# Polynomial-sketch attention and a rational-activation layer: 28 accumulating transfers, coefficients loaded by GpSimd, and a new order of all steps

## The chip, the cores and the metric

One core of a Trainium2 chip runs the whole program. The metric is the device time of one execution in microseconds, the median of several runs. Five engines work from queues of their own, each strictly in order: TensorE (PE, with its weight loads PEld), VectorE (DVE), ScalarE (ACT), GpSimd (POOL) and SyncE (SP). SP and POOL issue most of the DMAs.

## What is computed

Two stages in a row. The first is linear attention with a polynomial sketch, for 4 batches of 4 heads, 1088 positions and 32 channels. The second is a two-matrix layer (128 to 2048 to 128) whose activation is a cubic over a quadratic.

```python
def phi(x):
    a = np.einsum('rd,bhsd->bhsr', S1, x)          # r = 8
    b = np.einsum('rd,bhsd->bhsr', S2, x)
    return np.einsum('bhsi,bhsj->bhsij', a, b).reshape(*x.shape[:-1], r * r)
q_p, k_p = phi(q), phi(k)
kv = np.einsum('bhsf,bhsd->bhfd', k_p, v)
z = np.sum(k_p, axis=2)
num = np.einsum('bhsf,bhfd->bhsd', q_p, kv)
den = np.einsum('bhsf,bhf->bhs', q_p, z)[..., None] + 1e-06
x = (num / den)                                    # then (4352 tokens, 128)

h = x @ w_in                                       # 128 -> 2048
P = a[0] + a[1] * h + a[2] * h**2 + a[3] * h**3
Q = 1.0 + np.abs(b[0]) * np.abs(h) + np.abs(b[1]) * h**2
out = (P / (Q + 1e-06)) @ w_out                    # 2048 -> 128
```

## The kernel before

**An order written out by hand.** The string `ORDER` lists every step of the kernel, some 650 of them, by short names. The kernel walks through it once and emits each step's instructions. So each engine's queue is the list of its own steps in that order, and only waits between engines shape the time. A step's name gives its kind, its number, sometimes a part, and sometimes the engine (`a` for ScalarE, `d` for VectorE).

**Attention.** `Kb.…` are the steps of the keys of batch b: `T` turns them (VectorE), `s` forms the sketches (TensorE), `c` copies one factor out of PSUM, `f` multiplies the factors (VectorE), `p` multiplies with the values (TensorE), `k` keeps the result. `Qb.y.…` are those of the queries of one slice of a batch: `T`, `sk`, `c`, then `dw` and `dr` (written to DRAM and read back repeated, by SP's DMAs), `f` (VectorE), `p` (TensorE), `pl` (adds 1e-6 to the denominator), `r` (reciprocal, VectorE), `x` (quotient, VectorE), `b` (turned back by TensorE), `kk` (into the ring `xT`).

**The layer.** It is cut into 21 units (`UNITS`): a range of tokens and a range of the sixteen 128-wide slices of the hidden layer. Units 3 to 16 are 512 tokens by 8 slices, which is 4096 columns per partition; the first and the last ones are smaller. The steps of unit i, in the order of the data:

| step | engine | what it does |
|---|---|---|
| H | TensorE | h = w_in x, 1024 columns of PSUM at a time (two buffers `h_ps`) |
| E | ScalarE | evacuates them to `hh` in bf16 (three buffers) |
| U, W, Y | VectorE | u = abs(h) by a bit mask; w = b1 u + b0; w = w u, so that Q = 1 + w |
| L, X | ScalarE | ln of (w + 1 + 1e-6), then exp of its negative: r = 1/Q |
| S | VectorE | s = h r |
| P, V | VectorE | g = a3 h + a2; g = g h |
| G | VectorE | g = g s |
| Or, Os, Og | TensorE | gather: w_out times a0 with r, w_out times a1 with s, w_out with g |
| ST, OUT | ScalarE or VectorE, SP | out of PSUM, and to DRAM |

Three variants save work on one engine at another's cost:

- Units of `TWO` (6, 7, 8, 10, 12, 14, 15): behind V, step `A` adds a1 to g by an accumulating DMA that GpSimd issues, out of a DRAM tensor `ones` that holds a1 everywhere (fp32). Then the matmuls of Os aren't needed. There are two transfers of 512 KB per unit.
- Units of `SQ` and `ABS` (5, 9, 13): ScalarE squares h (`D`, with the root of b1 as scale) and forms b0 abs(h) (L530); `M` adds the two by an accumulating DMA. This takes the place of U, W and Y. `u` has one buffer, so the next unit's u waits until the transfer has read it.
- Units of `FOUR` (11, 13, 16, 17): VectorE forms s h and s h h (`B`, `C`) in place of P, V and G, and TensorE gathers four times (Or, Os, Om, On), the last two with weights scaled by a2 and a3 (steps w6 and w7).

So before there are 20 accumulating transfers, 14 for A and 6 for M. `w` and `r` and `s` have two buffers each, `g` four, the output tile two. P is done in halves of 2048 columns, as is D.

**The start.** SP issues the first loads (`I…`), among them the coefficients a and b (`I8`, L180 and L182). `AB0` takes the absolute of b and the root of b1 on ScalarE. `Z` steps are idle turns of TensorE on zeros.

Of the kernel before, what the change touches and what calls it, by code (L numbers as in the profile page):

```python
# [22 lines left out]
TWO = (6, 7, 8, 10, 12, 14, 15)  # L23
SQ = (5, 9, 13)
ABS = (5, 9, 13)
FOUR = (11, 13, 16, 17)
# [3 lines left out]
WIDE = {'U': 4096, 'W': 4096, 'Y': 4096, 'V': 4096, 'S': 4096, 'G': 4096, 'L': 4096}  # L30
# [8 lines left out]
I0 I11 I1 I2 K0.T0 SS0 Z10 K0.s0 K0.T1 K0.T2 K0.c0.a K0.f0 Q0.0.T Z3 K0.s1 Z3 Q0.0.sk I3 K0.p0 I8 F1.k I7 I9 I4 I5  # L39
K0.c1.a K0.f1 Q0.0.c.a Q0.0.f Q0.1.T K0.p1 K0.k0.d Q0.2.T K1.T0 Q0.1.sk Q0.0.p Q0.2.sk K1.s0 K1.T1 Q0.1.c.a  # L40
Q0.0.pl.a Q0.0.r Q0.0.x K1.T2 Q0.2.c.a Z2 Q0.0.b K1.s1 I6 I10 Q0.2.dw Q0.1.f K1.c0.a Q0.3.T Q0.0.kk.a H0.0 w2.d
K1.f0 AB0 w0.a w4.a K1.c1.d F1.q K1.f1 E0.0 U0.0 H1.0 Q0.3.sk E1.0 F1.v Q0.2.dr Q0.1.p H2.0 P0.0.d Q0.3.c.d W0.0
Q0.1.pl.d Y0.0 Q0.1.r U1.0 Q1.0.T V0.0 Q0.1.x W1.0 Q1.1.T w3.a P1.0.a E2.0 w1.a Y1.0 V1.0 H2.1 Q1.0.sk Q0.1.b
K1.p0 K1.p1 E2.1 Q1.0.c.a w5.a Q0.1.kk.a L0.0 P2.0.d Q0.2.f Q0.2.p Q0.2.pl.a K1.k0.a X0.0 Q1.2.T U2.0 Q0.2.r
Q1.1.sk Q1.2.sk Q0.3.dw F2.k Q1.0.dw Q0.2.x Q0.2.b Or0.0 W2.0 S0.0 V2.0 K2.T0 G0.0 Y2.0 Q0.2.kk.a L1.0 Q1.1.c.a
X1.0 H3.0 E3.0 H3.1 E3.1 K2.s0 K2.c0.a H3.2 L2.0 Q1.2.c.a E3.2 F2.q Q0.3.dr Q1.1.dw S1.0 K2.T1 P3.0.d G1.0 Q2.0.T
K2.f0 Q2.1.T H3.3 E3.3 Q0.3.f U3.0 K2.T2 W3.0 Q2.2.T Y3.0 Os0.0 H4.0 H4.1 Og0.0 Q2.0.sk Q1.0.dr Q1.2.dw Q1.1.dr
K2.s1 Q0.3.p X2.0 E4.0 P3.1.a H4.2 Q0.3.pl.d K2.c1.d Q1.0.f K2.f1 Q2.0.c.a E4.1 Q1.0.p H4.3 Q1.0.pl.d Q0.3.r
Q1.0.r Q0.3.x Q0.3.b L3.0 Q1.0.x S2.0 E4.2 Q0.3.kk.a Or1.0 Q1.0.b Os1.0 Os2.0 E4.3 Q1.2.dr F2.v Q2.0.dw Q1.0.kk.a
H5.0 H5.1 X3.0 E5.0 Q2.1.sk E5.1 Q2.1.c.a D5.0 Q2.2.sk H5.2 H5.3 E5.2 Q2.2.c.a E5.3 P4.0.d Q1.1.f U4.0 P4.1.d V3.0  # L50
W4.0 G2.0 Y4.0 S3.0 V4.0 Q1.2.f Og1.0 H6.0 Or2.0 F3.q F3.k Q2.1.dw Q2.0.dr Q2.2.dw Q1.1.p K2.p0 K2.p1 Q1.2.p Og2.0
H6.1 Q1.1.pl.d P5.0.d K2.k0.d Q1.1.r Q1.2.pl.d P5.1.d Q1.2.r Q3.0.T ST2.d Q1.2.x Q1.1.x D5.1 W5.0 E6.0 L4.0 Or3.0
H6.2 Q1.1.b Q1.2.b E6.1 X4.0 Q1.1.kk.a E6.2 H6.3 Os3.0 Q1.2.kk.a E6.3 Q3.0.sk G3.0 K3.T0 Q3.1.T P6.0.d Q2.0.f V5.0
S4.0 Q2.0.p Q3.1.sk Q3.0.c.a M5.0 L5.0 H7.0 E7.0 Og3.0 H7.1 H7.2 Q2.1.dr F3.v Q3.0.dw AW0 OUT2 Q2.2.dr X5.0 E7.1
K3.T1 Q2.0.pl.d G4.0 U6.0 P6.1.d W6.0 Q2.0.r Q3.2.T Y6.0 Q2.0.x S5.0 Q2.1.f V6.0 Q3.1.c.a E7.2 L6.0 Or4.0 H7.3
H8.0 E7.3 E8.0 Os4.0 Og4.0 H8.1 X6.0 E8.1 ST4.a Q3.1.dw Q3.0.dr OUT4 H8.2 H8.3 Or5.0 Q2.0.b K3.s0 Q2.1.p U7.0
P7.0.d W7.0 K3.T2 Y7.0 G5.0 P7.1.d S6.0 Q2.2.f E8.2 L7.0 Q2.0.kk.a E8.3 X7.0 H9.0 E9.0 H9.1 Q2.1.pl.a V7.0 U8.0
P8.0.d Q2.1.r Q3.0.f E9.1 K3.c0.a A6.0 D9.0 Os5.0 H9.2 H9.3 E9.2 E9.3 A7.0 Q2.1.x W8.0 K3.f0 Y8.0 K3.s1 K3.c1.a
S7.0 P8.1.d K3.f1 G6.0 Or6.0 Q2.1.b H10.0 Og5.0 H10.1 K3.p0 K3.p1 Q2.2.p D9.1 W9.0 E10.0 L8.0 E10.1 K3.k0.a X8.0
P9.0.d V8.0 P9.1.d Og6.0 H10.2 H10.3 E10.2 ST6.a E10.3 M9.0 Q2.1.kk.d V9.0 Q2.2.pl.d G7.0 P10.0.d S8.0 Q2.2.r  # L60
Q3.2.sk Q3.0.p U10.0 Q2.2.x H11.0 H11.1 L9.0 E11.0 Or7.0 Q2.2.b H11.2 Q3.0.pl.a Q3.2.c.d W10.0 Q3.0.r P10.1.d
Y10.0 E11.1 X9.0 A8.0 E11.2 H11.3 E11.3 Og7.0 Q3.0.x S9.0 U11.0 Q2.2.kk.d V10.0 Q3.0.b H12.0 H12.1 W11.0 G8.0
# [12 lines left out]
L20.0 Z4 Or18.0 OUT17 X20.0 Or19.0 Os18.0 Os19.0 Og18.0 Or20.0 S20.0 Os20.0 G19.0 Og19.0 G20.0 Og20.0 ST20 OUT20
# [4 lines left out]
def kernel(  # L80
# [81 lines left out]
    def early(n):  # L162
# [7 lines left out]
        elif n == 2:  # L170
            nc.sync.dma_start(out=q0[:, 0:QA], in_=q0_src[:, 0:QA])
        elif n == 3:
            load_v(0)
        elif n < 7:
            c, e = ((0, 512), (512, 1024), (1024, d_ff))[n - 4]
            nc.sync.dma_start(out=w_in_sb[:, c:e], in_=moe_w_in[:, c:e])
        elif n == 7:
            nc.sync.dma_start(out=q0[:, QA:S], in_=q0_src[:, QA:S])
        elif n == 8:
            nc.sync.dma_start(out=a_sb, in_=bass.AP(tensor=moe_a.tensor, offset=moe_a.offset,  # L180
                                                    ap=[[0, 128]] + list(moe_a.ap)))
# [63 lines left out]
    root1 = consts.tile([128, 1], FP, name="root1")  # L245
# [3 lines left out]
    a1, a2, a3 = a_sb[:, 1:2], a_sb[:, 2:3], a_sb[:, 3:4]  # L249
    w_sb = [big.tile([128, nf, d_model], BF, name=f"w_out_{i}") for i in range(3)] + [None, None]  # L250
    xT = big.tile([d_model, RING], FP, name="xT")
    if TWO:
        a1_sb = consts.tile([128, 128], FP, name="a1_sb")
        ones = dram.tile([128, 2048], FP, name="ones", bufs=1)
# [260 lines left out]
    def evac(i, part):  # L515
        c, ce = part * HW, min((part + 1) * HW, width(i))
        nc.scalar.copy(out=at(i, "hh", c, ce), in_=live[i]["h", part][:, :ce - c])  # L517
# [9 lines left out]
    def d_w(i, k, eng="d"):  # L527
        c = span(i, "W", k)
        if i in ABS:
            nc.scalar.activation(out=at(i, "u", *c), in_=at(i, "hh", *c), func=ACT.Abs, scale=ab0)  # L530
# [10 lines left out]
    def square(i, k):  # L541
        c = span(i, "D", k)
        nc.scalar.activation(out=at(i, "w", *c), in_=at(i, "hh", *c), func=ACT.Square, scale=root1)  # L543
# [127 lines left out]
    def w_part(x, eng):  # L671
        if x >= 6:
            t = feature_tile(x - 6)[:, 0:4].rearrange("p t h i j -> p (t h i j)").bitcast(BF)
            t = w_sb[x - 3] = t.rearrange("p (f d) -> p f d", f=nf)
            if eng == "d":
                nc.vector.tensor_scalar(out=t, in0=w_sb[2], scalar1=a_sb[:, x - 4:x - 3], scalar2=None, op0=AX.mult)
            else:
                nc.scalar.activation(out=t, in_=w_sb[2], func=ACT.Copy, scale=a_sb[:, x - 4:x - 3])
# [7 lines left out]
        if y == 2:  # L686
            copy(eng, o, t)
        elif eng == "d":
            nc.vector.tensor_scalar(out=o, in0=t, scalar1=a_sb[:, y:y + 1], scalar2=None, op0=AX.mult)
        else:  # L690
            nc.scalar.activation(out=o, in_=t, func=ACT.Copy, scale=a_sb[:, y:y + 1])

    def written(_):
        nc.sync.dma_start(out=ones.rearrange("p (a c) -> p a c", c=128),
                          in_=a1_sb[:, None, :].broadcast_to([128, 16, 128]))

    def absolute(_):
        if TWO:
# [56 lines left out]
```

## Time and profile before

| | us |
|---|---|
| median of 3 runs | 257.76 (257.49 to 258.58) |
| span of the profiled execution | 255.8 |
| TensorE busy in it | 249.8 |
| VectorE busy in it | 243.3 |
| ScalarE busy in it | 232.2 |
| accumulating transfers of ones, issue to landing, least / median / most | 6.9 / 9.7 / 12.4 |
| accumulating transfers of u, issue to landing, least / median / most | 4.6 / 6.9 / 9.1 |

The profile is of one execution. Its page gives each engine's busy time and share, the chain of work that ended last, and groups of instructions by line and form, as count, busy time in us, mean of one in ns, and idle time of the engine before them. A view by stretches gives busy time and count for each engine in each, then the granted TensorE clock (1.00 throughout), the share of the DMA engines and GB/s. A view in order of time gives start, duration, engine, line and tiles. TensorE's ends are modelled, so that a busy TensorE is not one at its peak. The span leaves out what lies around the program; the median of the runs is 1.96 us above it.

### The profile page before, as it was taken

How to read it: one execution, taken by the hardware profiler on the slowest of the kernel's cores; microseconds unless marked ns; L12 is line 12 of the kernel's file. 1: busy time of each engine (PE TensorE's matmuls, PEld its weight loads, DVE VectorE, ACT ScalarE, POOL GpSimd, SP SyncE). 2: the span in 40 equal slices, each digit the busy share in tenths (PEclk: the TensorE clock that was granted, in tenths of full speed). 3: DMA queues.
4: the chain of work that ended last, by engine and by line, in shares of the span. 5: the costliest groups of instructions: out<-in, count | busy, mean ns of one | idle time of the engine just before them, and what ended most of it. 6: DMA issues, size and time to landing. Idle time of an engine off the chain costs nothing.

```text
span 255.8 us, 6273 instructions
## 1 busy us (share of the span) xinstructions
PE 249.8 (98%) x2699; PEld 178.0 (70%) x2702; DVE 243.3 (95%) x242; ACT 232.2 (91%) x176; POOL 22.5 (9%) x46
## 2 busy tenths in 40 slices
PE   8999999999999999999999999999999999999993
PEld 3677746646866575666756656689566599999982
DVE  3699999999999999999999999999999999999992
ACT  2179989999999999999999999999899899999980
POOL 4000000000300040202200100220002020000000
PEclk9999999999999999999999999999999999999999
DMA  6999375649884669395995695399008575120100
GB/s 189 278 324 259 108 219 158 149 86 292 192 193 133 196 135 124 74 112 85 152 140 146 140 117 97 35 143 190 6 0 93 75 86 81 31 54 3 44 23 21
DMA packets 22618, 31.85 MB, mean 125 GB/s; under 512 B 2880, under 2 KB 15808, under 8 KB 22592
## 3 DMA queue, kind: packets, MB, share of 16 engines
q0 software_dynamic: 2880, 10.49, 30.1%
q1 hardware_dynamic: 19424, 20.90, 29.5%
q8 instruction: 21, 0.34, 0.5%
q10 hardware_dynamic: 288, 0.08, 0.1%
q14 instruction: 5, 0.04, 0.0%
HBM read 31.39 MB, written 4.26 MB: 139 GB/s over the span
## 4 chain that ended last, share of the span: by engine, by line
PE 96%; ACT 1%; DVE 0%; issue 0%; DVEq 0%
PE h_ps L511 47%; PE out_ps L616 34%; PE att_ps L426 3%; PE out_ps L197 3%; PE att_ps L330 2%; PE att_ps L454 2%; PE att_ps L299 1%; PE att_ps L366 1%; PE h_ps L376 1%; PE h_ps L299 1%; ACT hh L517 0%; ACT ln L575 0%; ACT w_out L265 0%; PE att_ps L197 0%; PE att_ps L322 0%
## 5 line engine op out<-in xcount | busy, mean ns | idle before, releaser
L511 PE MATMUL h_ps<-xT,w_in_sb 128*128 128x512 f32 (+1 forms) x320 | 126.2, 537 | 0.0
L511 PEld LDWEIGHTS h_ps<-xT,w_in_sb 128*128 128x128 f32 x320 | 57.5, 190 | 41.7 <-issue 36.6
L517 ACT CAST hh<-h_ps 128x1024 bf16<-128x1024 f32 x68 | 69.3, 1045 | 3.7 <-PE h_ps L511 2.2
L575 ACT ACTIVATE ln<-w 128x4096 f32<-128x4096 bf16 (+2 forms) x21 | 63.1, 3006 | 0.2 <-DVE w L553 0.2
L579 ACT ACTIVATE r<-ln 128x4096 bf16<-128x4096 f32 (+2 forms) x21 | 63.0, 2999 | 0.1
L583 DVE TENSOR_TENSOR s<-hh,r 128x4096 bf16<-128x4096 bf16 (+2 forms) x21 | 39.5, 1883 | 0.3 <-ACT r L579 0.2
L616 PEld LDWEIGHTS <-r 128*128 128x128 bf16 x544 | 31.7, 98 | 6.0 <-issue 5.1
L616 PEld LDWEIGHTS <-g 128*128 128x128 bf16 x544 | 31.4, 98 | 5.8 <-issue 5.1
L616 PE MATMUL out_ps<-w_out,r 128*128 128x128 bf16 x544 | 33.7, 219 | 0.0
L553 DVE TENSOR_TENSOR w<-w,u 128x4096 bf16<-128x4096 bf16 (+2 forms) x18 | 32.5, 1806 | 0.1
L571 DVE TENSOR_TENSOR g<-g,hh 128x4096 bf16<-128x4096 bf16 (+2 forms) x17 | 30.3, 1783 | 0.0
L587 DVE TENSOR_TENSOR g<-g,s 128x4096 bf16<-128x4096 bf16 (+2 forms) x17 | 30.2, 1781 | 0.0
L616 PEld LDWEIGHTS <-s 128*128 128x128 bf16 x448 | 25.9, 98 | 3.6 <-issue 3.4
L616 PE MATMUL out_ps<-w_out,g 128*128 128x128 bf16 x416 | 26.0, 219 | 0.0
L567 POOL DMA_DIRECT2D g<-ones x14 | 13.8, 1157 | 103.7 <-PE out_ps L616 39.1
L616 PE MATMUL out_ps<-w_out,s 128*128 128x128 bf16 x320 | 19.8, 219 | 0.0
L538 DVE TENSOR_SCALAR w<-u,b_abs 128x4096 bf16<-128x4096 bf16 (+2 forms) x17 | 19.3, 1136 | 0.0
L558 DVE TENSOR_SCALAR g<-hh,a_sb 128x2048 bf16<-128x2048 bf16 (+1 forms) x24 | 19.0, 793 | 0.0
L524 DVE TENSOR_SCALAR u<-hh 128x4096 uint16<-128x4096 uint16 (+2 forms) x17 | 17.3, 1015 | 0.1
L543 ACT ACTIVATE w<-hh,root 128x2048 bf16<-128x2048 bf16 x6 | 12.2, 2031 | 0.0
L549 POOL DMA_DIRECT2D w<-u x6 | 5.4, 1058 | 74.4 <-ACT u L530 74.4
L530 ACT ACTIVATE u<-hh,b_abs 128x4096 bf16<-128x4096 bf16 x3 | 11.1, 3713 | 0.0
(81 smaller groups left out, 207.1 us busy)
## 6 DMA issues: line engine op xcount, KB each, us to landing
g<-ones POOLq DMA_DIRECT2D x14, 512.0 KB, 9.7
w<-u POOLq DMA_DIRECT2D x6, 512.0 KB, 6.9
a_all<-sk_d SPq DMA_DIRECT2D x6, 352.0 KB
b_all<-sk_d SPq DMA_DIRECT2D x12, 176.0 KB
v_sb<-in_v_dram SPq DMA_DIRECT2D x12, 144.0 KB
k_sb<-in_k_dram SPq DMA_DIRECT2D x3, 544.0 KB
q_sb<-in_q_dram SPq DMA_DIRECT2D x3, 544.0 KB
out_dram<-out_sb SPq DMA_DIRECT2D x19, 64.0 KB
```

What stands on the lines that cost most here:

```text
L511: nc.tensor.matmul(t[:, (x - part * m) * tl:(x - part * m + 1) * tl], lhsT=w_in_sb[:, (f0 + x) * 128:(f0 + x + 1) * 128], rhs=xT[:, p:p + ...
L517: nc.scalar.copy(out=at(i, "hh", c, ce), in_=live[i]["h", part][:, :ce - c])
L524: nc.vector.tensor_scalar(out=at(i, "u", *c).bitcast(U16), in0=at(i, "hh", *c).bitcast(U16), scalar1=0x7FFF, scalar2=None, op0=AX.bitwise_and)
L538: nc.vector.tensor_scalar(out=at(i, "w", *c), in0=at(i, "u", *c), scalar1=ab1, scalar2=ab0, op0=AX.mult, op1=AX.add)
L553: nc.vector.tensor_mul(out=at(i, "w", *c), in0=at(i, "w", *c), in1=at(i, "u", *c))
L558: nc.vector.tensor_scalar(out=at(i, "g", *c), in0=at(i, "hh", *c), scalar1=a3, scalar2=a2, op0=AX.mult, op1=AX.add)
L571: nc.vector.tensor_mul(out=at(i, "g", *c), in0=at(i, "g", *c), in1=at(i, "hh", *c))
L575: nc.scalar.activation(out=ln_sb[:, :ce - c], in_=at(i, "w", c, ce), func=ACT.Ln, bias=1.0 + 1e-6)
L579: nc.scalar.activation(out=at(i, "r", c, ce), in_=ln_sb[:, :ce - c], func=ACT.Exp, scale=-1.0)
L583: nc.vector.tensor_mul(out=at(i, "s", *c), in0=at(i, "hh", *c), in1=at(i, "r", *c))
L587: nc.vector.tensor_mul(out=at(i, "g", *c), in0=at(i, "g", *c), in1=at(i, "s", *c))
L616: nc.tensor.matmul(outs[t0][:, m * 128:(m + 1) * 128], lhsT=z[:, m * 128:(m + 1) * 128], rhs=w, start=first and j == 0 and m == 0, stop=le ...
```

## The change

- `TWO` becomes (6, 8, 10, 11, 12, 13, 14, 15), `SQ` (5, 7, 9, 11, 13, 15), `FOUR` (16, 17); `ABS` goes. That makes 28 accumulating transfers: 16 of A and 12 of M.
- In units of SQ, u is now the plain abs(h) by VectorE's bit mask, the square's scale is the root of b1/b0, and the factor b0 enters in Ln as its scale (`scale0`).
- `ones` is bf16 instead of fp32. So that a1 may be rounded, `nearest` (steps KA0 to KA2) forms the ratio k of the rounded a1 to a1; a2 and a3 are multiplied by it, and the weights of g by its inverse.
- The coefficients are loaded by GpSimd's queue instead of SP's.
- P and D are done in one step of 4096 columns (except P of unit 3). E may be done by VectorE; seven of 68 are.
- `ORDER` is another one, throughout.

```diff
-TWO = (6, 7, 8, 10, 12, 14, 15)
-SQ = (5, 9, 13)
-ABS = (5, 9, 13)
-FOUR = (11, 13, 16, 17)
+TWO = (6, 8, 10, 11, 12, 13, 14, 15)
+SQ = (5, 7, 9, 11, 13, 15)
+FOUR = (16, 17)
+HALF = (3,)
...
-WIDE = {'U': 4096, 'W': 4096, 'Y': 4096, 'V': 4096, 'S': 4096, 'G': 4096, 'L': 4096}
+WIDE = {'U': 4096, 'W': 4096, 'Y': 4096, 'V': 4096, 'S': 4096, 'G': 4096, 'L': 4096, 'P': 4096, 'D': 4096}
...
-I0 I11 I1 I2 K0.T0 SS0 Z10 K0.s0 K0.T1 K0.T2 K0.c0.a K0.f0 Q0.0.T Z3 K0.s1 Z3 Q0.0.sk I3 K0.p0 I8 F1.k I7 I9 I4 I5
...
-S7.0 P8.1.d K3.f1 G6.0 Or6.0 Q2.1.b H10.0 Og5.0 H10.1 K3.p0 K3.p1 Q2.2.p D9.1 W9.0 E10.0 L8.0 E10.1 K3.k0.a X8.0
-P9.0.d V8.0 P9.1.d Og6.0 H10.2 H10.3 E10.2 ST6.a E10.3 M9.0 Q2.1.kk.d V9.0 Q2.2.pl.d G7.0 P10.0.d S8.0 Q2.2.r
...
+I0 K0.T0 I11 Z10 SS0 I1 K0.s0 Z1 K0.T1 K0.c0.d I8 AB0 RT0 K0.T2 K0.s1 Z3 K0.f0 I2 I3 Q0.0.T Q0.0.sk Q0.0.c.a K0.c1.d
...
+ST4.a V6.0 V7.0 E8.0.a Q2.2.dw H8.2 E8.2.a Q2.0.kk.a S6.0 Q2.1.p Or5.0 L7.0 H9.1 E9.1.a P8.0.d V8.0 H9.0 E9.0.a U8.0.d
+W8.0.d Q3.0.sk A6.0 Y8.0 K3.T0 G6.0 Q2.2.dr Q2.1.pl.a Q2.1.r Q2.1.x Og5.0 X7.0 A8.0 H9.3 H9.2 E9.3.a E9.2.a U9.0.d
+Q3.0.c.a P9.0.d K3.s0 H10.2 S7.0 D9.0 Q2.2.f F3.v M9.0 K3.s1 K3.c1.a L8.0 H10.3 E10.3.a Q3.1.sk Q3.2.T K3.c0.a Or6.0
+Os5.0 E10.2.d Og6.0 K3.f1 OUT2 Q3.1.c.a X8.0 H10.0 E10.0.a V9.0 ST6.a Q2.1.b Q2.1.kk.a K3.f0 H10.1 S8.0 G8.0 E10.1.a
...
-            nc.sync.dma_start(out=a_sb, in_=bass.AP(tensor=moe_a.tensor, offset=moe_a.offset,
+            nc.gpsimd.dma_start(out=a_sb, in_=bass.AP(tensor=moe_a.tensor, offset=moe_a.offset,
...
-        a1_sb = consts.tile([128, 128], FP, name="a1_sb")
-        ones = dram.tile([128, 2048], FP, name="ones", bufs=1)
+        a1_sb = consts.tile([128, 256], BF, name="a1_sb")
+        ones = dram.tile([128, 2048], BF, name="ones", bufs=1)
...
-    def evac(i, part):
+    def evac(i, part, eng="a"):
...
-        nc.scalar.copy(out=at(i, "hh", c, ce), in_=live[i]["h", part][:, :ce - c])
+        copy(eng, at(i, "hh", c, ce), live[i]["h", part][:, :ce - c])
...
-        if i in ABS:
-            nc.scalar.activation(out=at(i, "u", *c), in_=at(i, "hh", *c), func=ACT.Abs, scale=ab0)
-            return
...
-        nc.scalar.activation(out=at(i, "w", *c), in_=at(i, "hh", *c), func=ACT.Square, scale=root1)
+        nc.scalar.activation(out=at(i, "w", *c), in_=at(i, "hh", *c), func=ACT.Square, scale=root)
...
-        nc.scalar.activation(out=ln_sb[:, :ce - c], in_=at(i, "w", c, ce), func=ACT.Ln, bias=1.0 + 1e-6)
+        nc.scalar.activation(out=ln_sb[:, :ce - c], in_=at(i, "w", c, ce), func=ACT.Ln, bias=1.0 + 1e-6,
+                             scale=scale0 if i in SQ else 1.0)
...
+        by = k_inv if y == 2 else a_sb[:, y:y + 1]
...
     def absolute(_):
-        if TWO:
-            nc.gpsimd.tensor_copy(out=a1_sb, in_=a1.broadcast_to([128, 128]))
         nc.scalar.activation(out=b_abs, in_=b_sb, func=ACT.Abs)
-        if SQ:
-            nc.scalar.activation(out=root1, in_=ab1, func=ACT.Ln, bias=tiny)
-            nc.scalar.activation(out=root1, in_=root1, func=ACT.Exp, scale=0.5)
+        nc.gpsimd.tensor_scalar(out=scale0, in0=ab0, scalar1=1e-12, scalar2=None, op0=AX.max)
+
+    def nearest(n):
+        if n == 0:
+            nc.gpsimd.tensor_copy(out=a1_sb, in_=a1.broadcast_to([128, 256]))
+            nc.gpsimd.tensor_scalar(out=zero, in0=a1_sb[:, 0:1], scalar1=0.0, scalar2=None, op0=AX.is_equal)
+            nc.gpsimd.tensor_add(out=near[:, 0:1], in0=a1, in1=zero)
+            nc.gpsimd.tensor_add(out=near[:, 1:2], in0=a1_sb[:, 0:1], in1=zero)
+        elif n == 1:
+            nc.vector.reciprocal(out=near_inv, in_=near)
+        else:
+            nc.gpsimd.tensor_mul(out=a_k[:, 0:1], in0=near[:, 1:2], in1=near_inv[:, 0:1])
+            nc.gpsimd.tensor_mul(out=a_k[:, 1:2], in0=near[:, 0:1], in1=near_inv[:, 1:2])
+            nc.gpsimd.tensor_mul(out=a_k[:, 2:4], in0=a_sb[:, 2:4], in1=a_k[:, 0:1].broadcast_to([128, 2]))
+
+    def square_root(_):
+        nc.scalar.activation(out=ln_b[:, 0:1], in_=scale0, func=ACT.Ln)
+        nc.scalar.activation(out=ln_b[:, 1:2], in_=ab1, func=ACT.Ln, bias=tiny)
+        nc.scalar.mul(ln_b[:, 0:1], ln_b[:, 0:1], -0.5)
+        nc.scalar.activation(out=root, in_=ln_b[:, 1:2], func=ACT.Exp, scale=0.5, bias=ln_b[:, 0:1])
```

## The prediction

> **What bounds the kernel now.** I read the page first (busy shares and the chain that ended last), then the busy time by stretches of 30 us, then VectorE's instructions in order of time, then the groups by form for prices. The page:
>
> ```profile
> span 255.8 us, 6273 instructions
> ...
> PE 249.8 (98%) x2699; PEld 178.0 (70%) x2702; DVE 243.3 (95%) x242; ACT 232.2 (91%) x176; POOL 22.5 (9%) x46
> ...
> PE 96%; ACT 1%; DVE 0%; issue 0%; DVEq 0%
> ```
>
> By this page TensorE is the bound: 98% busy, and 96% of the chain. The stretches (columns PE, PEld, DVE, ACT, POOL) say more:
>
> ```profile
> 30.00:60.00 30.00, 30.00 (x216) 16.61 (x216) 29.94 (x38) 29.07 (x30) 0.00 (x0) 1.00 0.64 177
> ...
> 90.00:120.00 30.00, 30.00 (x297) 19.80 (x295) 29.68 (x24) 30.00 (x23) 5.73 (x6) 1.00 0.71 106
> ...
> 150.00:180.00 30.00, 30.00 (x367) 22.90 (x365) 29.78 (x24) 29.44 (x18) 3.52 (x4) 1.00 0.75 116
> ...
> 210.00:240.00 30.00, 30.00 (x384) 28.17 (x383) 29.89 (x19) 29.85 (x19) 0.00 (x0) 1.00 0.27 50
> ```
>
> From 30 to 240 us all three engines are full. VectorE lies idle 1.1 us in these 210. Of its 12.5 us outside busy time some 6.6 lie in the first 20 us and 4.6 behind its last work. So work taken from TensorE alone buys nothing: the end moves with VectorE's queue, and ScalarE's stands close behind it.
>
> **How VectorE's queue is priced.** Its instructions in order of time (start, duration):
>
> ```profile
> 171.03 0.69 DVE L267 COPY out_sb<-out_ps 128x512 f32<-128x512 f32 x1
> 171.63 2.29 DVE L592 TENSOR_TENSOR g<-s,hh 128x4096 bf16<-128x4096 bf16 x1
> 173.95 2.29 DVE L599 TENSOR_TENSOR s<-g,hh 128x4096 bf16<-128x4096 bf16 x1
> 176.16 0.17 DVE L435 TENSOR_SCALAR den<-att_ps 128x12 f32<-128x12 f32 x1
> ...
> 209.21 1.24 DVE L524 TENSOR_SCALAR u<-hh 128x4096 uint16<-128x4096 uint16 x1
> 210.49 1.34 DVE L538 TENSOR_SCALAR w<-u,b_abs 128x4096 bf16<-128x4096 bf16 x1
> 211.75 2.28 DVE L587 TENSOR_TENSOR g<-g,s 128x4096 bf16<-128x4096 bf16 x1
> ```
>
> An instruction that doesn't read what the one ahead of it wrote starts 0.08 to 0.09 us before that one's end: 173.95 + 2.29 - 176.16 = 0.08; 210.49 + 1.34 - 211.75 = 0.08. One that does starts 0.03 us after it: B11 at 171.63 + 2.29 = 173.92, C11 at 173.95; U16 at 209.21 + 1.24 = 210.45, W16 at 210.49. This holds all along VectorE's trace, wherever no other engine is waited for. So a step costs its duration less 0.085, and 0.12 more if it stands right behind the step that it reads. I call that a **pair**. Prices:
>
> ```profile
> L553 DVE TENSOR_TENSOR w<-w,u 128x4096 bf16<-128x4096 bf16 x12 | 27.4, 2280 | 0.1
> L538 DVE TENSOR_SCALAR w<-u,b_abs 128x4096 bf16<-128x4096 bf16 x12 | 16.1, 1341 | 0.0
> L524 DVE TENSOR_SCALAR u<-hh 128x4096 uint16<-128x4096 uint16 x12 | 14.7, 1221 | 0.1
> L558 DVE TENSOR_SCALAR g<-hh,a_sb 128x2048 bf16<-128x2048 bf16 x23 | 18.5, 804 | 0.0
> L311 DVE TENSOR_TENSOR k_p<-att_ps,b_sk 128x1024 f32<-128x1024 f32 x3 | 3.6, 1209 | 0.0
> L530 ACT ACTIVATE u<-hh,b_abs 128x4096 bf16<-128x4096 bf16 x3 | 11.1, 3713 | 0.0
> ...
> L543 ACT ACTIVATE w<-hh,root 128x2048 bf16<-128x2048 bf16 x6 | 12.2, 2031 | 0.0
> ```
>
> **The change on VectorE, step by step.**
> - Units 7, 11, 15 get the squared denominator and lose W and Y: 3 x (1.26 + 2.20) = -10.4.
> - Units 5, 9, 13 get U back from ScalarE: 3 x 1.14 = +3.4.
> - Units 11, 13 exchange B and C for V and G, four steps of 2.29 either way: 0.
> - P: before 23 halves at 0.72 and one quarter at 0.455, 17.0; after 12 whole steps (W's row stands for them, 1.255), two halves, three quarters, 17.9: +0.9.
> - Seven evacuations of 1024 columns from PSUM (E10.2, E12.1, E13.0, E14.1, E15.2, E16.0, E17.2) come from ScalarE. No row has this copy; the nearest, a product of the same width out of PSUM, is 1.21, and L689's cast of that width out of SBUF is 0.71: 7 x 0.63 to 1.13 = 4.4 to 7.9. I take 7.9, the row that reads PSUM too.
> - Small steps, by their rows less 0.085: U1, U20 (0.42 each), W1 (0.54), two kvz copies (0.29), two sketch copies (0.34, 0.32), five pieces of xT (2.1 together), four den (0.16), ST2 (0.39) and one more turn-out (0.69) leave, -4.9; the weight scalings w6, w7 (0.72) leave, -1.3; w1, w4, w5 (0.71) and a reciprocal (0.2) come, +2.0. Together -4.2.
>
> Sum without pairs: -2.4.
> - Pairs. Taking VectorE's steps alone out of each order, 10 of before stand right behind what they read. After has 54: P>V 12, S>G 9, U>W 9, r>x 8, W>Y 7, pl>r 4, others 5. 44 more at 0.12 is 5.3; some six lie in the first 20 us or the last 10, where VectorE waits anyhow, so 4.6 at least. I take +4.9.
>
> VectorE: **+2.5 us** (bounds -3.2, with the cheap evacuation and only half the pairs showing, and +2.9, with all 44).
>
> **ScalarE**, whose queue covers about 4 us of mid-kernel waits: three Abs of 3.71 leave, -11.1; squares go from six halves of 2.03 to six whole ones (the Abs row, 3.71), +10.1; seven evacuations leave, -7.3; weights, copies, den, U and W come, +8.6; the start's small ones +0.5. Ln of six units takes a per-partition scale: Ln with such a bias took 0.295 where Exp without took 0.203, so +0.5. Six more pairs at 0.13, +0.8. Sum some +1.6 with the overlap of more instructions: hidden, since VectorE's end moves further. If VectorE weren't later, up to 1.6 of it would show.
>
> **TensorE**: three groups of 32 gather matmuls fewer (two each in units 11 and 13, one more in unit 7), 96 x 0.056 = -5.4 (32 take 1.79 in the chain); eight idle turns fewer, -3.0. Worth nothing where VectorE is full.
>
> **Transfers.** 28 accumulating transfers instead of 20, issued two by two in 1.8 us on POOL, which is free. ScalarE's own work between the square and the logarithm that waits for the join was 14.8 to 15.4 us; it's now 10.8 to 13.4. Joins landed 4.6 to 9.1 us after issue, the second half issued 0.9 later, so 10.0 at worst: 0 for L, with 0.8 to spare. Behind a late join stand all evacuations in ScalarE's queue, then TensorE's two h_ps buffers. Of ones, V to G has 12.5 us of VectorE's work or more against 12.4 + 0.9 at worst, and the source is halved: 0 (0.8 once if not). U behind a join waits for it as well (one u buffer): 9.4 us or more of VectorE's work and the join's own issue; 0 to 0.6.
>
> The Trainium skill's "SBUF — State Buffer" (section "SBUF: two separate sides") says that descriptors of GpSimd's DMAs can't be written while VectorE runs in a two-port mode. The trace has issues of 0.86 to 1.99 us, so something holds them at times; by the rule joins would land later, which is the third rival below.
>
> **The start.** The coefficients' two DMAs go from SP (issued at 5.03 and 5.51) behind POOL's sketch weights, which end at 5.88; at 0.86 to 1.99 each they are issued by 7.6 to 9.9. On SP a_sb landed 3.4 us after its issue. Abs of b now stands ahead of Q0.0.c in ScalarE's queue, with four small ones (0.2 to 0.3) behind it: Q0.0.c starts at about 11.3 to 13, where it was 10.32. VectorE has Q0.1.T, Q0.2.T and two K0 copies to do meanwhile. So 0 to 1.5; I take +0.3. SP's later loads go 0.9 earlier. OUT8 goes to the end of SP's queue and keeps one of two out_sb buffers; ST10 to ST16 then wait for the store before them, which has some 15 us: 0.
>
> **Sum**: 255.8 + 2.5 + 0.3 = 258.6 for the profiled execution. The median of the runs, 257.76, is 1.96 above its span, so 257.76 + 2.8 = **260.6 us**.
>
> **Rivals.**
> 1. *Pairs cost nothing* in that queue (0.12): then -2.4 + 0.3, so 255.7, or up to 257.3 where ScalarE's +1.6 shows. For: the page's rows know no such price, and each is small. Against: ten of ten pairs before show it.
>    The Trainium skill, "VectorE: DVE Perf Modes" (The DRAIN you can't avoid), says that a semaphore after each of eight copies cost nothing extra. The trace disagrees by 0.12 us a pair.
> 2. *TensorE is the bound after all* (0.05): the chain says so. Then -5.4 alone: 252.4. Against it: VectorE idle 1 us in 210.
> 3. *A join lands late* (0.10): with more pairs, all six land like the worst of ones, 12.4 + 0.9 = 13.3. The gaps to L are 12.2, 12.4, 11.6, 13.4, 10.8, 10.8: 8.7 us of waits in ScalarE's queue, of which 4.9 are covered (4.0 that it waits now, 2.5 more behind VectorE, less 1.6). It decides from 10.8 us on: 260.6 + 3.8 = 264.4. For: the worst landing seen; against: joins landed sooner than ones each time.
> 4. *One cost is smaller* (0.11): evacuations at 0.63 give -0.7 in all, 257.1; half the pairs covered by waits give +0.5, 258.3. For: neither was seen in this place; against: the nearest rows.
>
> The forecast has 0.62, spread over 259.1 to 262.5. A measurement of this kernel tells 0.5% from no change, 1.3 us: slower is above 259.05, the forecast and rival 3, 0.72; faster is rival 2 and seven twelfths of rival 1, 0.12; the rest, 0.16, is the same. The range 256.4 to 263.5 leaves out rival 2, half of 1 and half of 3.
>
> **What would show it.** In VectorE's order of time: P8 then V8, S8 then G8 and U8, W8, Y8 with +0.03 us between, others -0.08; its busy time near 245 and its idle time in mid-kernel still about 1 us; E10.2 at 1.2 us; TensorE with some 8 us more idle time; Ln behind a join not waiting for a DMA. Wrong if VectorE shows idle time of several us in mid-kernel released by ScalarE or a DMA, or if pairs start like others.

## The result, and the profile after

The changed kernel takes **266.18 us** (median of 4 runs, 264.69 to 266.86), beside 257.62 (257.26 to 258.58) for the kernel before on the same chip: 1.0317 times as long, interval 1.0275 to 1.0358. That is 8.6 us slower. The profiled execution is the shortest of the four (264.69), with a span of 262.9 against 255.8: 7.1 of the 8.6 us can be looked at in it.

The page of the changed kernel, the lines that answer to those shown of before:

```profile
span 262.9 us, 6073 instructions
...
PE 249.0 (95%) x2597; PEld 172.0 (65%) x2598; DVE 244.7 (93%) x223; ACT 234.0 (89%) x184; POOL 32.9 (13%) x63
...
PEclk9999999999999799999999999999999999999999
...
DVE 44%; PE 16%; issue 15%; DMA 14%; ACT 8%; POOL 1%; SPq 1%; DVEq 0%; ACTq 0%
```

The chain, 96% TensorE before, now runs through VectorE and through DMAs (14%). One slice of 40 has a granted TensorE clock under 0.9. By stretches of 30 us (columns PE, PEld, DVE, ACT, POOL, clock, DMA share, GB/s):

```profile
30.00:60.00 30.00, 28.76 (x267) 16.63 (x266) 29.62 (x35) 27.24 (x30) 0.00 (x0) 1.00 0.57 164
60.00:90.00 30.00, 27.67 (x265) 16.71 (x264) 26.81 (x22) 27.15 (x21) 1.88 (x2) 0.94 0.62 149
90.00:120.00 30.00, 30.00 (x303) 19.82 (x302) 29.69 (x25) 28.89 (x22) 5.69 (x6) 1.00 0.78 153
...
150.00:180.00 30.00, 29.28 (x302) 20.36 (x300) 28.63 (x21) 29.97 (x19) 6.94 (x8) 1.00 0.70 142
...
210.00:240.00 30.00, 29.86 (x346) 26.70 (x345) 29.75 (x18) 29.89 (x15) 1.79 (x2) 1.00 0.30 61
```

VectorE is nearly full but for two stretches: 3.2 us are missing from 60 to 90, 1.4 from 150 to 180. Its list of waits (what it waited for: us in all, times, longest) names them:

```profile
DVE k_p L299 <- DMA k_sb<-in_k_dram: 4.2, 2, 2.7
DVE u L531 <- DMA w<-u: 3.0, 1, 3.0
DVE s L585 <- ACT r L581: 1.7, 2, 1.3
DVE a_all L419 <- ACT a_all L272: 1.4, 1, 1.4
```

The first and the last lie in the first 13 us, and VectorE waited about as long at the start before (5.6 us in all in the first 25 us, 5.9 now). The two in the middle are new, but for 0.2 us at an S step. This is the first of them in order of time, with only the rows that bear on it (start, duration, engine, line, and in brackets what ended the wait):

```profile
66.68 1.88 POOL L550 DMA_DIRECT2D w<-u  x2 [52.44 <-DVE g L559]
67.66 0.35 SPq L132 DMA_DIRECT2D q_sb<-in_q_dram  x1
68.05 0.46 SPq L128 DMA_DIRECT2D k_sb<-in_k_dram  x1
...
79.14 1.23 DVE L531 TENSOR_SCALAR u<-hh 128x4096 uint16<-128x4096 uint16 x1 [3.00 <-DMA w<-u]
80.41 1.35 DVE L539 TENSOR_SCALAR w<-u,b_abs 128x4096 bf16<-128x4096 bf16 x1
81.67 2.29 DVE L585 TENSOR_TENSOR s<-hh,r 128x4096 bf16<-128x4096 bf16 x1
...
84.05 1.93 ACT L272 CAST hh<-h_ps 128x1024 bf16<-128x1024 f32 x2 [1.20 <-DVE s L585]
85.11 5.40 PE L518 MATMUL h_ps<-xT,w_in_sb 128*128 128x512 f32 x8 [2.33 <-ACT hh L272]
```

It reads as a chain of five. POOL issues the two joining transfers of unit 5. One us later SP issues the queries and keys of the last batch, 544 KB each. The second join lands 11.7 us after its issue (the first took 5.7), and U6, which writes the one `u` buffer that the join reads, waits 3.0 us for it. Behind U6 in VectorE's queue stand W6 and then S4, the last reader of an `hh` buffer, so ScalarE's copies out of PSUM wait 1.2 and TensorE 2.3. Then eight matmuls of H take 5.40 us; without that wait eight take 3.49 (at 109.05 in the same trace's chain). The finer stretches (same columns) show why:

```profile
82.00:84.00 2.00, 0.78 (x28) 0.64 (x22) 2.00 (x2) 0.84 (x1) 0.00 (x0) 1.00 1.03 181
84.00:86.00 2.00, 0.89 (x2) 0.38 (x3) 2.00 (x1) 1.96 (x3) 0.00 (x0) 0.84 0.83 282
86.00:88.00 2.00, 2.00 (x4) 0.94 (x3) 2.00 (x3) 2.00 (x2) 0.00 (x0) 0.50 0.50 152
88.00:90.00 2.00, 2.00 (x5) 0.80 (x4) 2.00 (x4) 2.00 (x2) 0.00 (x0) 0.81 0.00 1
```

TensorE stands idle for 2.33 us, from 82.78 to 85.11. By the clock records of the trace the granted clock is then 0.50 from 85.34 to 88.76, which these stretches show as 0.84, 0.50 and 0.81.

The groups that stand for the prediction's prices (busy us, mean ns):

```profile
L274 DVE CAST hh<-h_ps 128x1024 bf16<-128x1024 f32 x7 | 8.4, 1204 | 0.0
L559 DVE TENSOR_SCALAR g<-hh,a_k 128x4096 bf16<-128x4096 bf16 x12 | 16.0, 1335 | 0.0
L576 ACT ACTIVATE ln<-w,scale 128x4096 f32<-128x4096 bf16 x6 | 22.4, 3738 | 1.1 <-DMA w<-u 1.1
```

**VectorE's account.** All rows of VectorE's timeline, added up: the end of the last one is its first start (0.85 us), the durations, the overlaps of neighbours (rows that start over 0.03 us before the end of the one ahead), the small gaps up to 0.12 us (pairs), and the longer waits. The three lower rows are experiments told below.

```
kernel                 end     durations  overlaps (rows)  small gaps (rows)  waits
before                 251.9   260.7      -17.4 (203)      +0.8 (17)           6.9
after                  259.2   256.5      -11.9 (145)      +2.4 (59)          11.3
e6 before, 17 pairs    254.1   260.0      -15.4 (190)      +1.2 (33)           7.5
e11 after, S4 first    257.5   256.5      -11.7 (144)      +2.6 (61)           9.3
e7 loads, start        255.6   256.4      -11.5 (142)      +2.4 (61)           7.5
```

From before to after: durations -4.2, overlaps and gaps +7.1, waits +4.4, together +7.3, which is the span's +7.1 within 0.2.

### The profile page after: what moved, and what is told of

It reads as the page before. It is cut to its first block, busy times and chain, and to the rows that moved or that the text cites. A ratio compares the mean times of both kernels' runs of the same rounds, so it can differ in the third digit from the quotient of the medians.

```text
span 262.9 us, 6073 instructions
## 1 busy us (share of the span) xinstructions
PE 249.0 (95%) x2597; PEld 172.0 (65%) x2598; DVE 244.7 (93%) x223; ACT 234.0 (89%) x184; POOL 32.9 (13%) x63
## 3 DMA queue, kind: packets, MB, share of 16 engines
q0 software_dynamic: 4096, 14.69, 30.6%
## 4 chain that ended last, share of the span: by engine, by line
DVE 44%; PE 16%; issue 15%; DMA 14%; ACT 8%; POOL 1%; SPq 1%; DVEq 0%; ACTq 0%
PE h_ps L518 9%; DMA w<-u 8%; DVE s L585 8%; DVE w L554 6%; DVE g L589 5%; PE out_ps L618 4%; DVE u L531 4%; DVE g L572 4%; DVE g L559 3%; DVE w L539 3%; ACT hh L272 3%; DVE hh L274 2%; DMA b_all<-sk_d 2%; DVE g L594 2%; DMA b_sb<-in_moe_b_dram 2%
## 5 line engine op out<-in xcount | busy, mean ns | idle before, releaser
L272 ACT CAST hh<-h_ps 128x1024 bf16<-128x1024 f32 x61 | 61.4, 1027 | 7.0 <-PE h_ps L518 5.8
L576 ACT ACTIVATE ln<-w 128x4096 f32<-128x4096 bf16 (+2 forms) x15 | 40.8, 2721 | 0.1
L589 DVE TENSOR_TENSOR g<-g,s 128x4096 bf16<-128x4096 bf16 (+2 forms) x19 | 34.7, 1830 | 0.3
L554 DVE TENSOR_TENSOR w<-w,u 128x4096 bf16<-128x4096 bf16 (+2 forms) x15 | 25.8, 1718 | 0.2
L550 POOL DMA_DIRECT2D w<-u x12 | 10.8, 1065 | 113.0 <-DVE g L559 52.4
L576 ACT ACTIVATE ln<-w,scale 128x4096 f32<-128x4096 bf16 x6 | 22.4, 3738 | 1.1 <-DMA w<-u 1.1
L544 ACT ACTIVATE w<-hh,root 128x4096 bf16<-128x4096 bf16 x6 | 22.3, 3711 | 0.1
L618 PEld LDWEIGHTS <-s 128*128 128x128 bf16 x352 | 20.3, 98 | 2.2 <-issue 1.1
L559 DVE TENSOR_SCALAR g<-hh,a_k 128x4096 bf16<-128x4096 bf16 (+2 forms) x17 | 19.2, 1131 | 0.0
L539 DVE TENSOR_SCALAR w<-u,b_abs 128x4096 bf16<-128x4096 bf16 (+2 forms) x13 | 14.8, 1137 | 0.3
```

The source lines that it names most:

```text
L272: nc.scalar.copy(out=out, in_=in_)
L539: nc.vector.tensor_scalar(out=at(i, "w", *c), in0=at(i, "u", *c), scalar1=ab1, scalar2=ab0, op0=AX.mult, op1=AX.add)
L554: nc.vector.tensor_mul(out=at(i, "w", *c), in0=at(i, "w", *c), in1=at(i, "u", *c))
L559: nc.vector.tensor_scalar(out=at(i, "g", *c), in0=at(i, "hh", *c), scalar1=a3, scalar2=a2, op0=AX.mult, op1=AX.add)
L589: nc.vector.tensor_mul(out=at(i, "g", *c), in0=at(i, "g", *c), in1=at(i, "s", *c))
L618: nc.tensor.matmul(outs[t0][:, m * 128:(m + 1) * 128], lhsT=z[:, m * 128:(m + 1) * 128], rhs=w, start=first and j == 0 and m == 0, stop=le ...
```

## The experiments

Two theories stood at the outset. Theory 1 is the prediction's own: VectorE's queue sets the end, and the pairs lengthen it. Theory 2 came from the trace above: the join of unit 5, landing late beside the batch loads. All edits below are edits of `ORDER` alone. Medians come with the kernel before on the same chip beside them: 257.75 us for e1 to e8, 257.95 for e9 and e10, 258.11 for e11 and e12.

### The pairs, taken away and put in by large rearrangement (e1, e2, e4)

In e1, 38 of VectorE's steps were moved so that 9 pairs are left of 54; in e4 the same with the batch loads of e3. In e2, 35 steps of the kernel before were moved so that it has 49 pairs instead of 10. Moves reach over some steps of other engines too. Two of e1's, cut out of the lines of `ORDER` as all such cuts below:

```diff
-P10.0.d V10.0
+P10.0.d G8.0 V10.0
...
-W2.0.d Y2.0 E3.3.a w5.d H4.3
+W2.0.d E3.3.a w5.d Y2.0 H4.3
```

> The changed kernel with 45 of its 54 pairs on VectorE parted: each time one neighbouring VectorE step is set between the two. Theory 1 (a step right behind the one that it reads costs 0.12 us more, in the queue that sets the end): 45 x 0.12 = 5.4 us less, 266.2 to about 260.8; VectorE's steps then start 0.085 us before the end of the one ahead, and its mid-kernel waits stay (3.0 us at U6, 1.7 us at S). Rival A (pairs are covered by waits for others, and it is the late join and ScalarE that set the end): 266 within 1 us, and what the pairs gave comes back as waits of S for ScalarE's r. In between, 262 to 264, would say that ScalarE's queue comes next.

> The kernel before with 39 pairs more (49 in all), made by moving VectorE steps by a few places; nothing else differs. Theory 1: 39 x 0.12 = 4.7 us more, 257.6 to about 262.3, with VectorE still idle only about 1 us in mid-kernel. Rival A: 257.6 to 258.6, since other engines cover it.

> Both at once: 45 pairs parted and the two loads later. Theories 1 and 2 together, if they add up: 266.2 - 5.4 - 3.0 = 257.8, and up to 260 if ScalarE's queue, 1.6 us longer than before and started later, sets the end then (S waiting for r by 2 us or more in sum). Rival A: like the run with the loads alone.

Measured: e1 **286.98** (285.64 to 287.91; ratio 1.1119, 1.1053 to 1.1186), e2 **268.41** (1.0391, 1.0338 to 1.0444), e4 **282.05** (1.0919, 1.0852 to 1.0986). No theory expected any of the three. VectorE's busy time went the way of theory 1: 244.7 to 241.4 in e1, 243.3 to 246.9 in e2. But VectorE's waits grew far more (e1):

```profile
DVE g L559 <- ACT hh L272: 6.5, 2, 4.2
DVE u L531 <- DMA w<-u: 5.6, 1, 5.6
DVE s L585 <- ACT r L581: 5.1, 4, 2.2
DVE den L442 <- PE att_ps L433: 5.0, 3, 2.0
```

A move that parts a pair puts one of VectorE's steps off. A likely reading is that others wait for that step, and VectorE later for them; the runs don't follow it step by step. In e1 all VectorE waits of 0.12 us and more come to 37.1 us, against 11.3. e4 is 4.9 us below e1: with the loads later, U's wait of 5.6 us for a join is gone there too. These runs don't measure a pair; they show how tight the order is.

### The batch loads, put later (e3)

```diff
-Q2.0.dw H6.3 F3.q ST2.a ... Os3.0 F3.k H7.0 Q3.1.T ... Q1.2.r Q2.1.dw H7.3 ... P6.0.d Q2.0.dr K3.T2
+Q2.0.dw H6.3 ST2.a ... Os3.0 H7.0 Q2.1.dw Q2.0.dr F3.q F3.k Q3.1.T ... Q1.2.r H7.3 ... P6.0.d K3.T2
```

F3.q and F3.k load the queries and keys of the last batch. In SP's queue they now stand behind Q2.1.dw and Q2.0.dr, just ahead of Q3.1.T, the first step that needs them.

> The changed kernel with the loads of the last batch's queries and keys (2 x 544 KB, issued 1 us behind unit 5's join) set behind the read-back of Q2.0 in SP's queue. Theory 2 (the join of unit 5 lands late because these loads share the DMA engines, and U6 waits 3.0 us for the one u buffer, then TensorE falls idle and loses its clock): the join lands within 10 us, U6 waits under 0.7 us, the granted clock stays at 1.00, and 266.2 becomes 262 to 263.5. Rival B (descriptors of the join are written late, or the join is slow in itself): it still lands at 11 to 12 us and the time stays within 1 us of 266.2.

Measured **262.59** (261.47 to 263.18; ratio 1.0158, 1.0102 to 1.0215): 3.6 us less than the changed kernel, as theory 2 expected. VectorE and SP around the join, which POOL issued at 67.02:

```profile
76.08 0.37 SPq L132 DMA_DIRECT2D q_sb<-in_q_dram  x1
76.41 1.22 DVE L531 TENSOR_SCALAR u<-hh 128x4096 uint16<-128x4096 uint16 x1
76.50 1.55 SPq L128 DMA_DIRECT2D k_sb<-in_k_dram  x1
```

The pair of transfers now landed 4.6 and 6.4 us after issue, where it took 5.7 and 11.7 beside the loads; U6 has no wait, and the granted clock is 1.00 in every stretch from 80 to 90 us. POOL's issue took 1.88 us both times. So the rival falls: without the loads beside it the join lands early.

### The same wait, with the loads left where they are (e11)

VectorE gets something else to do while the join is under way. X4, which makes r for S4, moves ahead of two small copies in ScalarE's queue with it.

```diff
-U6.0.d W6.0.d Q1.1.b Q1.1.kk.a Q2.2.c.a X4.0 S4.0 Y6.0
+X4.0 S4.0 U6.0.d W6.0.d Q1.1.b Q1.1.kk.a Q2.2.c.a Y6.0
```

> The changed kernel (266.2) with its loads where they are, but S4 of unit 4 (VectorE, 2.29 us, needs ScalarE's exponential, which ends at 78.1) ahead of U6 and W6 instead of behind them. The joining transfers of unit 5 still land at 79.1 beside the batch loads. Theory 2 (it is U6's wait for the one u buffer, and what stands behind it in VectorE's queue, that costs the time): VectorE works from 78.1 instead of 79.1, S4 is done 3.5 us earlier, the copies out of PSUM and TensorE's products behind S4 don't wait, TensorE keeps its clock: 262.5 to 264.5. Rival (the crowded DMA engines cost the time wherever VectorE stands): 266 as before, with the clock still falling near 85 us.

Measured **262.31** (261.76 to 263.11; ratio 1.0157, 1.0128 to 1.0186): 3.9 us less, a little better than expected.

```profile
78.42 2.29 DVE L585 TENSOR_TENSOR s<-hh,r 128x4096 bf16<-128x4096 bf16 x1 [1.48 <-ACT r L581]
80.00 3.72 ACT L576 ACTIVATE ln<-w,scale 128x4096 f32<-128x4096 bf16 x1 [0.98 <-DMA w<-u]
80.63 1.22 DVE L531 TENSOR_SCALAR u<-hh 128x4096 uint16<-128x4096 uint16 x1
...
86.00:88.00 2.00, 2.00 (x6) 0.86 (x5) 2.00 (x2) 2.00 (x1) 0.00 (x0) 1.00 0.53 151
```

The join lands as late as before (11.8 us after issue, and L5 still waits 0.98 for it). So the crowded DMA engines alone cost little: with the loads early (e11) the kernel is as fast as with the loads late (e3). It was VectorE standing still in front of U6, with S4 behind it, that cost the time. VectorE is still idle 1.48 us there, but S4 is done 3.3 us sooner and the clock stays at 1.00. Both changes at once weren't run, so what S4's new place is worth without a late join is open.

### Pairs by exchanging neighbours only (e6, e5, e12)

In e6, thirteen steps of the kernel before were moved by at most two places: 27 pairs instead of 10. For instance:

```diff
-W8.0 K3.f0 Y8.0
+W8.0 Y8.0 K3.f0
```

> The kernel before with thirteen of VectorE's steps each exchanged with a neighbour at most two places off, so that 27 instead of 10 steps stand right behind the step they read. Theory 1: 17 x 0.12 = 2.0 more than the kernel before, about 259.8. Rival (pairs cost nothing): as before, 257.8. Third reading (handovers upset): over 260.5, with new waits of VectorE for other engines of more than 1 us together.

Measured **259.95** (259.50 to 260.93; ratio 1.0089, 1.0060 to 1.0118): +2.2 us, where 2.0 were expected. In VectorE's order of time, e6 first, then before at the same place:

```profile
94.76 1.34 DVE L537 TENSOR_SCALAR w<-u,b_abs 128x4096 bf16<-128x4096 bf16 x1
96.13 2.29 DVE L552 TENSOR_TENSOR w<-w,u 128x4096 bf16<-128x4096 bf16 x1
98.34 0.37 DVE L291 STREAM_TRANSPOSE k_p<-k_sb 128x192 f32<-128x192 f32 x1
```

```profile
94.43 1.35 DVE L538 TENSOR_SCALAR w<-u,b_abs 128x4096 bf16<-128x4096 bf16 x1
95.69 0.38 DVE L292 STREAM_TRANSPOSE k_p<-k_sb 128x192 f32<-128x192 f32 x1
95.98 2.25 DVE L553 TENSOR_TENSOR w<-w,u 128x4096 bf16<-128x4096 bf16 x1
```

Y starts 0.03 after W's end where it reads W's result at once (96.13 against 94.76 + 1.34); with the small transpose between, each row starts 0.09 before the end of the one ahead. In the account, overlaps and small gaps cost 2.4 us more (13 overlaps fewer, 16 gaps more), 0.6 more is waited, and the durations are 0.7 less. "Pairs cost nothing" is out: its 257.8 lies below the interval.

The opposite way, from e3 (e5: ten exchanges, 41 pairs of 54 left) and from e7 (e12: twelve exchanges from unit 7 on, where its expectation counts eleven; 38 left):

```diff
-Q3.1.x P13.0.d V13.0
+P13.0.d Q3.1.x V13.0
```

> The changed kernel with the batch loads later (e3, 262.6), and ten of VectorE's steps each exchanged with the one next to it, so that 41 instead of 54 steps stand right behind the step they read. Nothing is moved by more than one place in the order. Theory 1 (a pair costs 0.12 us): 13 x 0.12 = 1.6 less, 261.0. Rival (pairs cost nothing): 262.6. Third reading, after the large rearrangements: even a shift by one step upsets the handovers to ScalarE and TensorE, then more than 262.6, with VectorE's idle time (not its gaps at pairs) larger than in e3.

> e7 (261.0) with VectorE's steps from unit 7 on exchanged with a neighbour at most two places off, eleven exchanges, so that 38 instead of 54 steps stand right behind the step they read. Theory 1: 16 x 0.12 = 1.9 less, 259.1. Rival (pairs cost nothing): 261. Third reading (e5's: the steps put off are waited for by other engines): 260.5 or more, with the smaller gaps at pairs seen in the trace and new waits of VectorE that eat them.

Measured: e5 **262.87** (262.02 to 264.92; ratio 1.0202, 1.0164 to 1.0241), so nothing gained on e3; e12 **264.39** (263.58 to 264.57; 1.0225, 1.0195 to 1.0255), 3.4 lost on e7. The gaps did shrink (overlaps and small gaps together some 0.7 us less in e5, 1.4 in e12), and new waits ate it, the third reading of both. So the price of a pair is shown by the time of a run in one direction only; in the other it is seen in the trace. In e12 most of the new waits come after 210 us, for example:

```profile
223.22 0.69 DVE L274 COPY out_sb<-out_ps 128x512 f32<-128x512 f32 x1 [1.60 <-PE out_ps L618]
224.65 1.23 DVE L531 TENSOR_SCALAR u<-hh 128x4096 uint16<-128x4096 uint16 x1 [0.74 <-ACT hh L272]
```

### The start (e7), and the output weights (e8)

e7 is e3 with `AB0` and `RT0` moved behind `Q0.2.c.a`; e8 is e7 with `w6.a`, which stood between `L10.0` and `X10.0`, moved behind the latter.

```diff
-L10.0 A11.0 Os7.0 w6.a Q3.0.x Og7.0 E12.3.a Q3.1.f X10.0
+L10.0 A11.0 Os7.0 Q3.0.x Og7.0 E12.3.a Q3.1.f X10.0 w6.a
```

> e3 with ScalarE's two first coefficient steps (abs of b and the roots, which wait 8 to 9 us for the load of b_sb that GpSimd issues) moved behind ScalarE's share of the first copy into a_all. Theory A (VectorE's wait of 1.4 to 2.6 us for that copy is on the path): 0.8 to 2 us less, 260.6 to 261.8. Rival (the first 12 us end with the loads of the first batch whatever ScalarE does): 262.6.

> e7 with ScalarE's rounding of the output weights for the second pass (w6, 2.0 us) moved from ahead of the logarithm of unit 10 to behind its exponential. VectorE waits there 1.3 to 2.1 us for the exponential (s reads r). Theory B (that wait is local): 1.2 to 2 us less than e7, about 259 to 260. Rival (ScalarE is full there, and the 2.0 us only come up again at the next unit): as e7 within 0.4.

Measured: e7 **260.99** (260.09 to 261.80; ratio 1.0120, 1.0087 to 1.0152), e8 **260.82** (260.25 to 262.83; 1.0132, 1.0095 to 1.0168).

e7's size is theory A's, but its trace isn't. VectorE no longer waits for the copy into `a_all` (2.6 us in e3), yet it waits for the next things instead, and U3 starts at 38.30 us where it started at 38.53: 0.23 gained. The larger part comes 90 us later, at the join of unit 9. In e3 its second half lands 12.2 us after issue and ScalarE's logarithm waits for it:

```profile
133.19 3.71 ACT L576 ACTIVATE ln<-w,scale 128x4096 f32<-128x4096 bf16 x1 [1.81 <-DMA w<-u]
```

In e7 it lands after 10.1 us, that wait is gone, and X9 ends 2.0 us sooner (0.4 of it was there before the logarithm):

```profile
130.74 3.82 ACT L576 ACTIVATE ln<-w,scale 128x4096 f32<-128x4096 bf16 x1
```

Why it lands sooner there is open; so the 1.6 us between e3 and e7 (whose intervals overlap) aren't shown to be the start's.

e8 is the rival's. VectorE's wait at S10 (1.06 us in e7) is gone, and U12 behind it waits 1.17 for ScalarE's copies instead:

```profile
155.33 2.01 ACT L680 ACTIVATE k_p<-w_out,a_k 128x2048 bf16<-128x2048 bf16 x1
...
159.67 1.23 DVE L531 TENSOR_SCALAR u<-hh 128x4096 uint16<-128x4096 uint16 x1 [1.17 <-ACT hh L272]
```

ScalarE is full there, and the 2 us of weights are paid in either place.

### Work given to ScalarE (e9, e10)

```diff
-ST8.d ... ST10.d ... Q3.2.kk.d
+ST8.a ... ST10.a ... Q3.2.kk.a
```

```diff
-E12.1.d ... E14.1.d ... E16.0.d
+E12.1.a ... E14.1.a ... E16.0.a
```

The first is of the kernel before (e9), the second of e7 (e10).

> The kernel before with three of VectorE's small steps given to ScalarE: two turn-outs out of PSUM (ST8, ST10; 0.69 us on VectorE, 0.62 on ScalarE by their rows) and one copy of xT (0.82). They lie between 155 and 207 us, where ScalarE is idle for 2.9 us in all. Theory 1 (the end moves with VectorE's queue): 1.5 to 1.9 us less, 255.9 to 256.3. Rival (TensorE, at 97 to 98 per cent, sets the end): 257.8. Third reading (ScalarE's queue is as tight there, its next copies out of PSUM come later): more than 258.

> e7 (261.0) with three of the seven copies out of PSUM that the change gave to VectorE given back to ScalarE (E12.1, E14.1, E16.0: 1.2 us each on VectorE, 1.0 on ScalarE). Theory 1 in its plain form (VectorE alone sets the end): 3 x 1.13 = 3.4 less, 257.6. Rival (ScalarE is as full there, 29.8 to 30.0 of each 30 us from 90 to 240): 260.5 to 262, with VectorE idle some 3 us more for ScalarE's r and hh.

Measured: e9 **270.55** (269.32 to 271.91; ratio 1.0486, 1.0450 to 1.0522), e10 **265.24** (264.33 to 268.13; 1.0283, 1.0242 to 1.0324), so 12.6 and 4.2 us worse; the third reading of e9, and more than the rival of e10. In e9, ScalarE stands from 169.0 to 175.1 us before one copy of 0.58 us, for TensorE's gather (in the kernel before, VectorE made this copy at 171.03), and D, L and X behind it are late, then S12 on VectorE:

```profile
175.09 0.58 ACT L264 COPY out_sb<-out_ps 128x512 f32<-128x512 f32 x1 [6.07 <-PE out_ps L615]
...
188.43 2.29 DVE L582 TENSOR_TENSOR s<-hh,r 128x4096 bf16<-128x4096 bf16 x1 [11.10 <-ACT r L578]
```

In e10 VectorE's waits grow from 7.5 us to 17.5, the larger new ones after 30 us for ScalarE's r and hh (2.69, 2.57, 2.13); its profiled execution is the longest of six (268.13). ScalarE's idle time in a stretch (2.9 us from 155 to 207 in the kernel before) wasn't room for work here. e9 was to test whether VectorE's queue sets the end of the kernel before; since the copies come late on ScalarE, it doesn't decide that.

No version tried is faster than the kernel before.

## Why the prediction was wrong

The sign was right, and the two reasons given for it, VectorE's work and the pairs, are found in the trace at about the size written; the sum wasn't right. It said +2.8 us and a top of 263.5; the kernel takes 8.6 us more. The prediction's own sign of being wrong came: VectorE stands idle in mid-kernel, 3.0 us for a DMA and 1.7 for ScalarE.

**What held.**
- *The steps' durations.* The sum without pairs, -2.4, counts 0.085 less for each of 19 instructions fewer; as durations that is -4.0. Measured: -4.2. The evacuation took 1.204 us in the mean against 1.21 from the row chosen (the upper end), P 1.335 against 1.341, and Ln with a scale 3.738, 0.10 more than the 3.637 of the nine 4096-wide ones without (+0.6 for six, +0.5 written).
- *The pairs.* 44 more were to cost 4.6 to 5.3. Overlaps and small gaps rose by 7.1 us; less the 1.6 of 19 fewer overlaps, 5.5. In the changed kernel's trace a P of 1.33 us begins at 154.81 and its V at 156.18, 0.04 after its end; e6 is the test of it by itself, 2.2 against 2.0. Rival 1 falls with it. The Trainium skill's "VectorE: DVE Perf Modes" (The DRAIN you can't avoid) says that a semaphore after each of eight copies cost nothing extra. It doesn't say that one copy read another's result, and VectorE's dependent neighbours do cost 0.12 us each here.
- *VectorE's sum* was to be +2.5; by the account it is -4.2 + 7.1 = +2.9. In e7, where VectorE waits only 0.6 us more than before, what is left is 260.99 - 257.75 = 3.2 us.
- *TensorE* has less to do, and that bought nothing; rival 2 falls. Its weight loads fell from 178.0 to 172.0 us; the page's matmul time, whose ends are modelled, only from 249.8 to 249.0. That its idle time rose by 7.9 us, near the 8 foretold, is luck: 7.1 of it is the longer span.
- *The start* was to be +0.3: in the first 25 us VectorE waits 5.9 us instead of 5.6.

**What failed is the step "Transfers".** It took the landings of before, 4.6 to 9.1 us, and the second issue 0.9 later, as a bound ("10.0 at worst"), and priced U behind a join at "0 to 0.6". The join of unit 5 landed 11.7 us after the second issue. The step had U6's cover right (9.4 us of work; U6 could have started at 76.1, 9.5 after POOL's issue began), and the one `u` buffer. It didn't ask what else moves at that time: the new order issues two batch loads of 544 KB one us behind the join. e3 takes them away and the same transfers land after 4.6 and 6.4 us; e11 leaves them and fills the wait, and the time comes back as well. So 3.6 to 3.9 of the 8.6 us are this one wait, with S4, the copies, TensorE's wait and the lowered clock behind it. That size comes from the medians. The profiled executions show less than half of it: spans of 262.9, 261.3 and 261.1 us, so 1.6 to 1.8. The other runs of the changed kernel were 0.9 to 2.2 us longer than the profiled one and have no trace; the two longest had lower granted clocks (0.990 and 0.985, against 0.993), so they may have lost the clock a second time, which isn't shown.

Rival 3 had a late join as its mechanism, but at L in ScalarE's queue and from "the worst of ones"; in the changed kernel L waited 1.1 us in all. U was the place that decided, on an engine with no idle time left. The rule named with that rival, the Trainium skill's "SBUF — State Buffer" (SBUF: two separate sides), would show as a long issue on POOL. The trace has the pair in question at 1.88 us, the other five joins at 1.77 or 1.78, and in e3 the same 1.88 before landings of 4.6 and 6.4 us; so it isn't what made this join late.

**A smaller failure: ScalarE's +1.6 was called hidden**, since VectorE's end moves further. ScalarE's busy time rose by 1.8 (232.2 to 234.0), and VectorE waited 1.7 us for r at two S steps, 1.5 more than before. An engine that ends earlier on the whole can still be late at one handover: the two weights of 2.00 us stand in its queue ahead of X10, behind which one of the two waits lies (1.25 us). e8 and e10 show that there is no room behind them either.

By size: 3.6 to 3.9 at U6, 3.2 VectorE's work and pairs (2.5 written), and 1.6 between e3 and e7, which is not settled between the start, the join of unit 9 and ScalarE.

## What to carry to other kernels

A landing time measured in one order is no bound for another: before a transfer is priced, list what every other queue issues while it is under way, and look at the first reader of its buffer on an engine that has no idle time. When several engines are full, the duration of a step can be the smaller part of its price: three copies of 0.7 to 0.8 us, moved to an engine with "free" time, cost 12.6 us, and moving 38 steps cost 20.8, because other engines wait for steps at their places. A small systematic price (0.12 us for a step right behind the one that it reads) is best seen by exchanging neighbours and by adding up overlaps and gaps in the trace, not by rearranging.

## What the runs showed of the hardware that wasn't expected

- Two accumulating transfers of 512 KB landed 4.6 and 6.4 us after issue without the two loads of 544 KB behind them (e3), 5.7 and 11.7 with them, and again 5.7 and 11.8 in e11: the second transfer takes most of the delay.
- After TensorE's gap of 2.33 us the granted clock was 0.50 for 3.41 us; eight matmuls took 5.40 us instead of 3.49. With one such loss in 263 us the mean clock is still 0.993.
- Within each of the fourteen traces the changes of the clock lie whole multiples of 3.41 us apart (in e4: 6.79, 13.62, 20.45, 61.41, 64.82, 180.88, 184.29). Cut into pieces of 3.41 us on that grid, every piece at full clock in which TensorE was busy 1.41 us or less was followed by one at 0.50, and every one with 1.71 or more by one at 1.00; of the two between, the one with 1.54 kept the clock and the one with 1.67 lost it. So it matters where a gap falls: 2.35 us without a matmul cost the clock in e4 (58.11 to 60.46, inside one piece) and not in e1 (56.72 to 59.07, across two).
